# A planned kernel for attention and two expert stages: other task durations and start rules in the planner, the ranking in four tasks, early transposes in other PSUM banks

## The chip, the cores and the metric

The kernel runs on one core of a Trainium2 chip. The metric is the device time of one execution in microseconds (us); lower is better. The kernel before takes 797.78 us (median of 3 runs, 797.66 to 799.06).

## The reference

Three stages follow each other, all in float32. `q`, `k`, `v` have 4 batches, 8 heads, 576 positions and 64 numbers for each head; there are 2304 tokens of 512 numbers.

```python
scores = q @ k.T / sqrt(64) - 2.0**-(head + 1) * abs(i - j)   # only 0 <= i - j < 128
x = softmax(scores) @ v                    # back to (2304, 512)
h = x @ w_in                               # 512 -> 2048
x = (h - tanh(h)) @ w_out                  # 2048 -> 512
logits = cos(x, expert_emb) / tau          # 8 experts
e = argmax(logits); gate = softmax(logits)[e]
out = gate * (relu(x @ w1[e]) @ w2[e])     # for each token, its own expert; 512 -> 1024 -> 512
```

## The kernel before

**The work.** Tokens are in 18 blocks of 128, and two blocks make one of 9 groups (`g`). Attention of a block is done in four quarters of two heads each (`quarter`). The middle stage runs in 72 steps (`step`): one step is one group with two of the 16 column blocks of `w_in` and the rows of `w_out` that answer to them. The first four steps belong to group 0, the next eight to group 1, then come the other four of group 0, and eight for each later group. When a group is done, `route` finds its experts and scatters its rows into a bucket for each expert in HBM. Then eight experts follow (`moe2`, `expert`), with their own weights. Products are made in two or three parts (a rounded high part and the rest), so each float32 operand is split once: the high part is copied by ScalarE (ACT) or VectorE (DVE), the rest is a subtraction on VectorE or GpSimd (POOL).

**The order.** Nothing runs in the order in which it is written. Every piece of work is a task of `Plan`: the engines that could do it with a duration for each, a due time, the keys that it reads and writes, and a PSUM bank that it takes or frees. `Plan.order` is a list scheduler that runs while the program is built: it keeps a time for each engine, takes again and again the task that can start first (ties go to the earlier due time), and puts it on the engine that is expected to finish first. The tasks, sorted by planned start, are then written out in that order, and each engine works through its own list in order. So a duration in the plan doesn't change an instruction; it changes where in its engine's list the instruction stands. On the chip, semaphores hold each instruction until its operands are there.

**A quarter.** `scores` (PE, into the banks `sc0` and `sc1`, or `acc0` and `acc1` for odd quarters below `NALT`), `soft` (VectorE: bias and row minimum, L498), `exp` (ACT, L512). For the first four blocks (`early`) the probabilities are transposed on PE into the single bank `misc` (`tr_pe`, L533), copied out (`tr_out`, L537) and multiplied with `v` (`pv_f`, L547). For all later blocks they are split into float16 parts (`s_hi`, `s_lo`), transposed by a DMA that SP issues (`tr`, L527: `pt<-ph`), and multiplied on PE (`pv`, L558). `x_out` transposes a finished block on PE into `misc` (L645), and ACT (L652) and VectorE (L653) copy it to `xT`, which the first product of a step (`g1`, L693) reads. The second product is `g2` (L717); it reads `gh` and `gl` (L706, L710).

**The routing.** `route` splits a block into three bfloat16 parts (L791, L796), transposes them by one DMA (`turn`, L800: `x3T<-x`) and multiplies them with the embeddings on PE (`lg3`, L805). `choose` and `settle` rank the experts by their number of tokens with some 20 small VectorE instructions in one task each (`ranking`); SP reads the result for the addresses of the experts' weights.

The planner's model of a transfer that SP issues:

```python
free[e] = st + 0.5                     # SP is free again
pipe = max(pipe, st + 1.1) + eng[e]    # the DMA pipe, with the task's own time
end = pipe + 1.0                       # landed
```

Of the kernel before, what the change touches and what calls it, by code (L numbers as in the profile page):

```python
# [24 lines left out]
NT = B * S  # L25
DM = H * D
FF = 2048
E = 8
# [13 lines left out]
LOENG = {"DVE": 0.69}  # L42
LEAD = 2
WLEAD = 1
# [3 lines left out]
NALT = 8  # L48
ALPHA = 1.0
# [21 lines left out]
class Plan:  # L71
# [4 lines left out]
    LAT = {"PE": 0.3, "SP": 0.0, "SW": 0.0}  # L76
# [4 lines left out]
    def add(self, eng, fn, due, r=(), w=(), take=None, free=None):  # L81
# [16 lines left out]
        self.tasks.append((eng, fn, due, deps, take, free))  # L98

    def order(self, places):  # L100
# [8 lines left out]
        pipe = 0.0  # L109
# [3 lines left out]
        while cand:  # L113
# [8 lines left out]
            for n in cand:  # L122
                eng, fn, due, _, take, _ = T[n]
# [5 lines left out]
                fin = {e: max(free.get(e, 0.0), r0) + c + ALPHA * load.get(e, 0.0) for e, c in eng.items()}  # L129
                e = min(fin, key=fin.get)  # L130
                st = max(free.get(e, 0.0), r0)
# [6 lines left out]
            eng, fn, _, _, take, rel = T[n]  # L138
            if take:
                avail[take].remove(min(avail[take]))  # L140
            if e == "SP":
                free[e] = st + 0.5
                pipe = max(pipe, st + 1.1) + eng[e]
                end = pipe + 1.0
            elif e == "SW":
                free["POOL"] = max(free.get("POOL", 0.0), st) + 1.04
                free[e] = st + eng[e]
                end = st + eng[e] + 2.0
            else:
                end = free[e] = st + eng[e]  # L150
            lat = self.LAT.get(e, 0.15)
# [14 lines left out]
class Builder:  # L166
# [64 lines left out]
    def consts(self, P):  # L231
# [8 lines left out]
        for h in range(H):  # L240
            P.add({"DVE": 0.2} if h < 2 else {"POOL": 0.5}, lambda e, h=h: self.eng(e).tensor_scalar(
# [67 lines left out]
    def weight(self, P, kind, f, due):  # L309
# [35 lines left out]
        P.add({"DVE": 0.47, "ACT": 0.62}, top, due, r=[raw], w=[zk])  # L345
        P.add({"DVE": 0.69}, rest, due, r=[raw, zk, "at"], w=[wf])
        P.add({"ACT": 0.62, "DVE": 0.47}, hi, due, r=[wf, "at"], w=[raw, (key, 0)])
# [6 lines left out]
    def qk_half(self, P, b, hf, due):  # L354
# [27 lines left out]
        sub = {"POOL": 1.23, "DVE": 0.6}  # L382
        if b >= NF - 1:
            k, kh = ("k", b, hf), ("kh", s, hf)
            P.add({"SP": 0.73}, lambda e: load("k"), due - 2, r=["at"], w=[k, "stk"])
            P.add({"ACT": 0.52}, kcopy, due, r=["at", k, "stk"], w=[kh])
            P.add(sub, ksub, due, r=["at", kh, "stk"], w=[("kl", s, hf)])
        if b >= NF:
            q, qn = ("q", b, hf), ("q", n)
            P.add({"SP": 0.73}, lambda e: load("q"), due - 2, r=["at"], w=[q, "stq"])  # L390
            P.add({"ACT": 0.52}, qcopy, due, r=["at", q, "stq"], w=[qn])
            P.add(sub, qsub, due, r=["at", qn, "stq"], w=[("ql", n)])
# [28 lines left out]
    def v_half(self, P, b, hf, due):  # L421
# [5 lines left out]
        def load(e):  # L427
# [4 lines left out]
        sub = {"DVE": 0.34, "POOL": 0.69}  # L432
        P.add({"SP": 0.36}, load, due - 2, r=["at"], w=[("vst", n)])
        P.add({"ACT": 0.31}, lambda e: nc.scalar.copy(out=v[0], in_=st["v"]), due, r=["at", ("vst", n)],
              w=[("vt", s, hf, 0)])
        P.add(sub, lambda e: self.eng(e).tensor_tensor(out=st["v"], in0=st["v"], in1=v[0], op=ALU.subtract), due,
              r=["at", ("vt", s, hf, 0)], w=[("vst", n)])
# [1063 lines left out]
```

## Time and profile before

| what | value |
|---|---|
| time, median of 3 runs | 797.78 us |
| the profiled execution | 795.44 us, of which 793.8 us are its span from the first to the last instruction |
| PE (TensorE) busy in the span | 762.9 us, 96% |
| VectorE, ScalarE, GpSimd busy | 569.4, 419.8, 239.1 us |
| granted clock of TensorE, mean of the span | 0.994 of 2.4 GHz |

All times below are from the start of that span. "Busy" is the time in which an engine has an instruction in work. PE's instructions overlap, so a short hole between two of them can disappear in its busy time; weight loads (PEld) are listed apart. A wait is idle time of an engine just before an instruction, put down to what released it.

### The profile page before, as it was taken

How to read it: one execution, taken by the hardware profiler on the slowest of the kernel's cores; microseconds unless marked ns; L12 is line 12 of the kernel's file. 1: busy time of each engine (PE TensorE's matmuls, PEld its weight loads, DVE VectorE, ACT ScalarE, POOL GpSimd, SP SyncE). 2: the span in 40 equal slices, each digit the busy share in tenths (PEclk: the TensorE clock that was granted, in tenths of full speed). 3: DMA queues.
4: the chain of work that ended last, by engine and by line, in shares of the span. 5: the costliest groups of instructions: out<-in, count | busy, mean ns of one | idle time of the engine just before them, and what ended most of it. 6: DMA issues, size and time to landing. Idle time of an engine off the chain costs nothing.

```text
span 793.8 us, 15243 instructions
## 1 busy us (share of the span) xinstructions
PE 762.9 (96%) x5237; PEld 678.1 (85%) x5237; DVE 569.4 (72%) x1538; ACT 419.8 (53%) x953; POOL 239.1 (30%) x256
## 2 busy tenths in 40 slices
PE   6899999999999999999999999999999999999994
PEld 4789899897988989889989888889779989899993
DVE  5989889977796786887887875875466665666320
ACT  5887875564554544555555633564255545545220
POOL 3231238554353343344424321331200210210210
PEclk9999999999999999999999999999999999999998
DMA  8984278764363363364364433572367656665000
GB/s 308 415 349 123 81 205 239 149 146 96 98 143 86 67 147 87 74 146 101 84 124 108 87 61 92 148 239 81 105 231 232 217 178 203 201 199 175 30 29 30
DMA packets 127416, 117.34 MB, mean 148 GB/s; under 512 B 87885, under 2 KB 91981, under 8 KB 127200
## 3 DMA queue, kind: packets, MB, share of 16 engines
q1 hardware_dynamic: 124304, 106.81, 48.9%
q0 software_dynamic: 3024, 9.46, 3.2%
q8 instruction: 43, 0.70, 0.4%
q14 instruction: 45, 0.37, 0.2%
HBM read 85.81 MB, written 16.56 MB: 129 GB/s over the span
## 4 chain that ended last, share of the span: by engine, by line
PE 61%; DMA 13%; DVE 11%; issue 9%; ACT 2%; POOL 1%; SPq 1%; POOLq 0%; DVEq 0%; ACTq 0%
PE h L693 18%; PE acc L717 16%; PE he L1092 9%; PE y L1127 7%; DMA out<-yo,ix 4%; PE o L558 3%; PE y L1123 2%; DMA rawo<-in_w_out 2%; PE sc L476 2%; DMA x3T<-x 2%; DVE gl L710 2%; DMA est<-in_w 2%; DMA pt<-ph 1%; DMA stk<-in_k 1%; DVE sc L498 1%
## 5 line engine op out<-in xcount | busy, mean ns | idle before, releaser
L693 PE MATMUL h<-xT,wi 128*128 128x256 f32 x1728 | 226.3, 285 | 0.0
L693 PEld LDWEIGHTS h<-xT,wi 128*128 128x128 f32 x1728 | 217.6, 192 | 5.4 <-issue 1.0
L717 PE MATMUL acc<-wo,gh 128*128 128x512 f32 x576 | 184.6, 402 | 0.5 <-DVE x2row L757 0.5
L717 PE MATMUL acc<-wo,gl 128*128 128x512 f32 x288 | 113.1, 393 | 0.0
L717 PEld LDWEIGHTS acc<-wo,gh 128*128 128x128 f32 x576 | 99.0, 189 | 15.0 <-DVE x2row L757 0.7
L698 ACT ACTIVATE t<-h 128x512 f32<-128x512 f32 x72 | 43.0, 598 | 93.4 <-PE h L693 85.5
L1127 PE MATMUL y<-eo,ge 128*128 128x512 f32 x336 | 88.8, 399 | 0.3 <-ACT ge L1108 0.3
L512 ACT ACTIVATE p<-sc,mx 128x256 f32<-128x256 f32 (+1 forms) x128 | 59.3, 464 | 43.1 <-DVE mx L498 37.7
L1152 POOL DMA_INDIRECT out<-yo,ix x23 | 23.5, 1020 | 189.9 <-ACT yo L1148 40.2
L710 DVE TENSOR_TENSOR gl<-t,gh 128x512 fp32r<-128x512 f32 x72 | 67.5, 937 | 5.7 <-ACT gh L706 4.8
L1127 PEld LDWEIGHTS y<-eo,ge 128*128 128x128 f32 x336 | 59.5, 188 | 10.6 <-ACT ge L1108 0.6
L498 DVE CUSTOM_DVE_ANT_0 sc<-sc,bias 128x256 f32<-128x256 f32 (+1 forms) x136 | 49.5, 373 | 23.7 <-PE sc L476 20.0
L1025 DVE TENSOR_TENSOR eo<-est,eo 128x512 fp32r<-128x512 f32 x61 | 44.6, 736 | 29.5 <-ACT eo L1021 27.9
L717 PEld LDWEIGHTS acc<-wo,gl 128*128 128x128 f32 x288 | 54.1, 188 | 12.7 <-DVE gl L710 0.7
L1021 ACT CAST eo<-est 128x512 fp32r<-128x512 f32 x64 | 39.5, 620 | 36.9 <-PE y L1123 18.4
L701 DVE TENSOR_TENSOR t<-h,t 128x512 f32<-128x512 f32 x72 | 49.4, 687 | 13.3 <-ACT t L698 13.2
L1114 DVE SCALAR_TENSOR_TENSOR ge<-he,ge 128x256 fp32r<-128x256 f32 x104 | 28.7, 316 | 40.8 <-ACT ge L1108 39.8
L1092 PEld LDWEIGHTS he<-xA,ei 128*128 128x128 f32 x384 | 54.2, 188 | 2.5
L1092 PE MATMUL he<-xA,ei 128*128 128x288 f32 (+2 forms) x384 | 56.1, 295 | 0.0
L1108 ACT ACTIVATE ge<-he 128x288 fp32r<-128x288 f32 (+2 forms) x56 | 23.1, 414 | 61.5 <-PE he L1092 55.9
L522 POOL TENSOR_TENSOR ph<-p,ph 128x512 f16<-128x512 f32 (+1 forms) x33 | 38.3, 1160 | 56.9 <-ACT ph L517 41.6
L1092 PEld LDWEIGHTS he<-xT,ei 128*128 128x128 f32 x384 | 53.4, 189 | 2.1
(208 smaller groups left out, 1325.9 us busy)
## 6 DMA issues: line engine op xcount, KB each, us to landing
est<-in_w SPq DMA_DIRECT2D x128, 256.0 KB
rawi<-in_w_in SPq DMA_DIRECT2D x16, 511.8 KB
rawo<-in_w_out SPq DMA_DIRECT2D x16, 511.8 KB
stk<-in_k SPq DMA_DIRECT2D x30, 256.0 KB
stq<-in_q SPq DMA_DIRECT2D x28, 256.0 KB
bucket<-in_c_pad SPq DMA_DIRECT2D x8, 771.0 KB
xe<-bucket SPq DMA_DIRECT2D x17, 257.0 KB
vst<-in_v SPq DMA_DIRECT2D x30, 128.0 KB
```

What stands on the lines that cost most here:

```text
L498: nc.vector.tensor_tensor_reduce(out=x, in0=x, in1=self.bias[:, h, c0:c1], scale=-0.125, scalar=mx[:, 1:2] if m else 3.0e38, op0=ALU.add, ...
L512: nc.scalar.activation(out=v["p32"][:, jj * W:(jj + 1) * W], in_=x, func=AF.Exp, scale=-1.0, bias=v["mx"][jj][:, 0:1], accum_out=self.sums ...
L522: self.eng(e).tensor_tensor(out=ph[:, 2 * W:4 * W], in0=v["p32"][:, 0:2 * W], in1=ph[:, 0:2 * W], op=ALU.subtract)
L693: nc.tensor.matmul(h3(v["h"], f2), lhsT=w[:, a, k, :], rhs=xT[c][:, :, k, :], start=(k == 0 and n == 0), stop=(k == KD - 1 and n == 2))
L698: nc.scalar.activation(out=v["t"], in_=v["h"].rearrange("p a b -> p (a b)"), func=AF.Tanh)
L701: nc.vector.tensor_tensor(out=v["t"], in0=v["h"].rearrange("p a b -> p (a b)"), in1=v["t"], op=ALU.subtract)
L710: self.eng(e).tensor_tensor(out=v["gl"], in0=v["t"], in1=v["gh"].bitcast(F32), op=ALU.subtract)
L717: nc.tensor.matmul(self.acc[g, t], lhsT=v[a][:, c0:c0 + 128], rhs=self.w["o", fs[f2]][:, c, :], start=(first and f2 == 0 and n == 0), stop ...
L1021: nc.scalar.copy(out=t[:, 0, :], in_=v["x"])
L1025: self.eng(eng).tensor_tensor(out=t[:, 1, :], in0=v["x"], in1=t[:, 0, :].bitcast(F32), op=ALU.subtract)
L1092: nc.tensor.matmul(h[:, 0:N], lhsT=w[:, a, c0:c0 + 128], rhs=xT()[b][:, k, 0:N], start=(k == 0 and n == 0), stop=(k == KD - 1 and n == 2))
L1127: nc.tensor.matmul(y[t], lhsT=gt(f, a)[:, (t - ts[0]) * 128:(t - ts[0] + 1) * 128], rhs=self.w["o", f0 + f][:, b, :], start=(f == 0 and n ...
```

## The change

It edits the planner and the tasks' declarations. The arithmetic and the number of instructions stay as they are.

- Nearly all task durations get other values, most of them larger: a step's `g1` 1.285 to 1.425, its `g2` 0.643 to 0.69, `tanh` 0.48 to 0.63, the subtractions 0.60 to 0.72, the weight casts on ACT 0.62 to 0.81, `pv` 0.53 to 0.56.
- Tasks get a `late` value. The two kinds of DMA transposes (`tr` and `turn`) have `late=2.5`: what they produce is planned as ready 2.5 later, and SP is planned as taken for 1.25. For other transfers SP is planned as free after 0.4 in place of 0.5.
- Tasks get a `port` flag. While the last planned GpSimd task runs, a flagged task isn't planned to start on VectorE. Flagged are the weights' `top`, `rest` and `hi`, the subtractions of `qk_half` and `v_half`, `recip`, a step's `lo` (`gl`), and in `route` the scaling and the casts.
- The latency between tasks is 0.05 in place of 0.15, and 0.2 in place of 0.3 behind PE.
- Odd quarters below 8 transpose into the bank `h1`, and `x_out` of blocks 0 and 1 into `h0`; these banks are used by `g1` from the first steps on.
- `choose` and `settle` are cut into several tasks with their own due times: the keys, `ranks`, `order`, `places`, and what follows. The instructions are the same.

```diff
-LOENG = {"DVE": 0.69}
+LOENG = {"DVE": 0.72}
+LATE = 2.5
+NOWN = 8
+NXO = 2
-    LAT = {"PE": 0.3, "SP": 0.0, "SW": 0.0}
+    LAT = {"PE": 0.2, "SP": 0.0, "SW": 0.0}
...
+                at = {e: max(free.get(e, 0.0), r0) for e in eng}
+                if port and "DVE" in at and pool[0] <= at["DVE"] < pool[1]:
+                    at["DVE"] = pool[1]
+                fin = {e: at[e] + c + ALPHA * load.get(e, 0.0) for e, c in eng.items()}
...
-                free[e] = st + 0.5
-                pipe = max(pipe, st + 1.1) + eng[e]
-                end = pipe + 1.0
+                free[e] = st + (1.25 if late else 0.4)
+                pipe = max(pipe, st + 1.0) + eng[e]
+                end = pipe + 0.9
...
-            lat = self.LAT.get(e, 0.15)
+                if e == "POOL":
+                    pool = (st, end)
+            lat = self.LAT.get(e, 0.05) + late
...
-            v["tp"] = self.misc()
+            v["tp"] = self.misc(f"h{own}" if own is not None else "misc")
...
-        P.add({"SP": 0.5 if one else 0.9}, tr, due, r=["at", ("ph", a % 2), ("ph", a % 2, 1)], w=[("pt", a % 2)])
+        P.add({"SP": 0.7 if one else 1.2}, tr, due, late=LATE, r=["at", ("ph", a % 2), ("ph", a % 2, 1)], w=[("pt", a % 2)])
...
+        own = 0 if b < NXO else None
+        hb = [("h", own)] if own is not None else []
...
-            v["ps"] = self.misc()
+            v["ps"] = self.misc(f"h{own}" if hb else "misc")
...
-            P.add({"PE": 1.285}, lambda e, f2=f2: g1(f2), due, ...
+            P.add({"PE": 1.425}, lambda e, f2=f2: g1(f2), due, ...
-        P.add({"DVE": 0.6}, lo, due - 20, r=["t", gh], w=[gl])
+        P.add({"DVE": 0.72}, lo, due - 20, r=["t", gh], w=[gl], port=True)
...
-            P.add({"SP": 1.35}, lambda e, t=t: turn(t), due, r=[("x3", n) for n in range(3)], w=["x3T", ("wz", 1)])
+            P.add({"SP": 1.55}, lambda e, t=t: turn(t), due, late=LATE, r=[("x3", n) for n in range(3)], w=["x3T", ("wz", 1)])
...
-        P.add({"DVE": 2.4}, pick, due, r=["cps", "con", "small"], w=["big", "first", ("ids", 0)], free="misc")
+        P.add({"DVE": 0.4}, start, due, r=["cps", "con", "small"], w=["first", "rank"], free="misc")
+        self.ranking(P, due, 0)
+        P.add({"DVE": 0.8}, pick, due, r=["rank"], w=["big", "first"])
...
+        P.add({"DVE": 1.0}, ranks, due, r=["con"], w=["rank"])
+        P.add({"DVE": 0.7}, order, due, r=["con"], w=["rank"])
+        P.add({"DVE": 0.5}, places, due, r=["rank"], w=[("ids", n)])
...
-        P.add({"DVE": 2.6}, fix, due, r=["cps", "con", "small"], w=["first", "cap", ("ids", 1)], free="misc")
+        P.add({"DVE": 0.4}, start, due, r=["cps", "con", "small"], w=["first", "rank"], free="misc")
+        self.ranking(P, due, 1)
+        P.add({"DVE": 1.3}, fix, due + 1, r=["rank"], w=["cap", "key2"])
+        P.add({"DVE": 0.2}, least, due + 1, w=["cap"])
```

## Rows read from the trace of the kernel before

**Rows 1.** Windows: span in us, then busy us (instructions) of each engine, PEclk, DMA share, GB/s.

```profile
0.00:60.00 60.00, 49.77 (x336) 40.39 (x337) 47.54 (x146) 44.44 (x119) 20.78 (x48) 1.00 0.94 357
60.00:540.00 480.00, 471.81 (x3470) 422.24 (x3469) 390.83 (x1054) 269.63 (x629) 183.79 (x177) 1.00 0.51 123
540.00:783.00 243.00, 241.00 (x1436) 215.53 (x1434) 131.01 (x340) 105.09 (x206) 33.52 (x31) 1.00 0.47 150
...
20.00:40.00 20.00, 16.13 (x132) 14.28 (x132) 17.98 (x52) 17.96 (x45) 5.39 (x6) 1.00 1.03 415
```

**Rows 2.** Waits of PE from 60 to 545 us: total us, times, longest us.

```profile
PE o L558 <- DMA pt<-ph: 2.7, 3, 1.7
PE misc L805 <- DMA x3T<-x: 2.3, 4, 0.9
PE o L558 <- DVE gl L710: 1.1, 1, 1.1
PE misc L1365 <- DVE cum L873: 0.7, 1, 0.7
PE acc L717 <- DVE x2row L757: 0.5, 1, 0.5
PE misc L805 <- DVE xT L653: 0.5, 1, 0.5
PE misc L846 <- DVE oh L836: 0.3, 1, 0.3
```

**Rows 3.** Waits of PE in the first 60 us.

```profile
PE sc L470 <- DMA kf<-in_k: 4.3, 1, 4.3
PE sc L470 <- ACT p L512: 3.1, 3, 1.7
...
PE misc L645 <- ACT ptf L537: 0.6, 1, 0.6
PE misc L533 <- DVE xT L653: 0.4, 1, 0.4
```

**Rows 4.** Windows of 2 us from 294 to 300 us; PEclk is third from the end.

```profile
294.00:296.00 2.00, 1.67 (x26) 1.67 (x27) 0.94 (x6) 0.00 (x0) 1.08 (x1) 0.95 0.96 307
296.00:298.00 2.00, 2.00 (x11) 2.00 (x11) 1.58 (x13) 0.22 (x1) 0.00 (x0) 0.50 0.73 142
298.00:300.00 2.00, 2.00 (x17) 1.96 (x16) 0.00 (x0) 0.15 (x1) 0.00 (x0) 0.70 0.00 0
```

**Rows 5.** The chain that ended last, in order of time: start us, us, what.

```profile
151.68 4.92 DMA pt<-ph
...
183.31 4.76 DMA x3T<-x
...
223.86 2.83 DMA stq<-in_q
...
453.63 3.08 DMA pt<-ph
...
510.10 1.78 DVE x L796
```

**Rows 6.** Instructions on the tile pt, their ns (least/median/most), and who waited for it.

```profile
L527 SPq DMA_TRANSPOSE pt<-ph x56: 1189/1232/2398, 81.9 to 483.1; - x56
...
  PEld L558: 7.4, 10
```

**Rows 7.** Instructions on the tile gl: VectorE's subtraction of a step, ns least/median/most.

```profile
L710 DVE TENSOR_TENSOR gl<-t,gh x72: 661/692/1811, 41.8 to 539.2; 128x512 fp32r<-128x512 f32 x72
```

**Rows 8.** Timeline of VectorE at two borders between groups: start us, us.

```profile
151.15 0.68 DVE L653 TENSOR_TENSOR xT<-misc,xT 128x512 fp32r<-128x512 f32 x1
206.65 0.68 DVE L653 TENSOR_TENSOR xT<-misc,xT 128x512 fp32r<-128x512 f32 x1
```

**Rows 9.** Timeline of PE at the same two borders: the next group's first product.

```profile
152.28 1.92 PE L693 MATMUL h<-xT,wi 128*128 128x256 f32 x14
...
208.81 1.59 PE L693 MATMUL h<-xT,wi 128*128 128x256 f32 x12
```

## The prediction before the change was built

> **What bounds the kernel now.** I read the windows first, by stage. Between 60 and 540 us PE is busy for 471.8 of 480 us, from 540 to 783 us for 241.0 of 243 us; in the first 60 us it is idle for 10.2 us, and after 783 us the span has 10.8 us in which the last rows leave the chip [rows 1]. So TensorE is the bound, and a new order of the same instructions can win only PE's holes: 8.2 us in the middle, 2.0 us in the experts, and some of the 10.2 us ahead. Nothing in the change touches the last 10.8 us.
>
> Next come PE's own waits, which say whose the holes are. In the middle seven kinds make 8.1 of the 8.2 us [rows 2]. Three waits for the transposes of the probabilities (2.7 us, the longest 1.7) and four for those of the routing (2.3 us) are 5.0 us. VectorE's `gl` makes 1.1 us, its `cum` 0.7, `x2row` 0.5, `xT` 0.5 and `oh` 0.3. At the start, 4.3 us wait for the first load and 3.1 us for the first exponentials; only 0.6 + 0.4 = 1.0 us are waits of a transpose for the shared bank `misc` [rows 3].
>
> Then the granted clock, which busy time doesn't show. It is 0.95, 0.50 and 0.70 in three windows of 2 us from 294 us on, and 1.00 in all the stages around [rows 4, 1]. A level of 0.50 is 1.2 in place of 2.4 GHz. PE had just stood still for its longest wait in the middle, the 1.7 us for `pt` [rows 2]. The price is 2 x (0.05 + 0.50 + 0.30) = 1.7 us, on top of the hole.
>
> **The change, part by part.** No instruction is added or removed, so each part is worth what the new order does to these holes.
>
> *Later transposes.* The old plan lets `pt` land 1.1 + 0.9 + 1.0 = 3.0 us after SP starts; the new one says 1.0 + 1.2 + 0.9 + 2.5 = 5.6 us. The chain shows 4.92 and 3.08 us for `pt`, and 4.76 us for `x3T` [rows 5]. So 3.0 was too little by up to 1.9 us, and 5.6 is above all of them. SP is held for 1.19 to 2.40 us by one transpose [rows 6], where the old plan said 0.5 and the new one says 1.25. The plan will put at least one more product ahead of `pv` and `lg3`. The margin of 2.5 us is above the longest of these waits, 1.7 and 0.9 us [rows 2], so all seven could close. I take 4.0 of the 5.0 us, because the operands of a transpose can be late too. Bounds: nothing, if the holes only move; and 7.4 us, the idle time of the weight loads that wait for `pt` alone [rows 6], if PE's busy time hides part of the loss.
>
> A rule of the Trainium skill speaks against this part. The Trainium skill, Advanced Engine Details and Errata, section X-Bar Transpose (TRN2), says that such transposes are as fast as ordinary transfers. A plain load took 2.83 us in the same chain, against 3.08 and 4.92 [rows 5]: one of the two transposes agrees, the other doesn't. By the rule the old 3.0 was right, the added 2.5 corrects nothing, and this term would be 0.
>
> *The clock.* With the wait of 1.7 us gone there is nothing here that slows the clock: 1.7 us. Bounds 0 and 1.7.
>
> *True durations and the port rule.* VectorE's subtraction for `gl` takes 692 ns at the median and up to 1811 [rows 7], where the old plan has 0.6. The new plan has 0.72 and doesn't start it beside GpSimd. That bears on the `gl` wait (1.1 us) and, by better times in general, on the other 2.0 us of [rows 2]. I take 1.0 of the 3.1 us, between 0 and 3.1: the flag is on only some of VectorE's work. The routing's own subtraction, which has no flag, took 1.78 us at 510 us [rows 5].
>
> The Trainium skill, SBUF — State Buffer, section Who interferes with whom, says that a VectorE instruction with two SBUF inputs and a GpSimd instruction that reads SBUF block each other for a whole instruction. The 1811 ns agree in kind [rows 7]. By that rule the unflagged subtractions go on colliding, as with my 1.0; a plan that flagged them all could aim at 3.1.
>
> *Banks.* The odd early quarters and the first two `x_out` no longer queue for `misc`: 1.0 us [rows 3]. From 20 to 40 us VectorE is busy for 17.98 and ACT for 17.96 of 20 us [rows 1], so the two copy engines, not the banks, limit the start. Bounds 0 and 5.9 us, which is the idle 10.2 us without the first load's 4.3. The new readers of `h0` and `h1` stand ahead of `g1`, which needs their results anyway; no wait is added that isn't there by the data.
>
> *Ranking in tasks.* The VectorE work is the same; other subtractions may slip in between. It lies where PE's whole idle time is the 0.7 us behind `cum` [rows 2] and the 2.0 us of the experts [rows 1]. I take 0; the bounds are a loss and a gain of 2.0 us. SP's reading of the ranks waits for the same instructions as before. If the cover goes, the experts' loads behind that reading are late next.
>
> *What goes the other way.* The old plan has little room at the borders between groups. At two of them `xT` is done at 151.83 and 207.33 us, and the next group's `g1` starts at 152.28 and 208.81 [rows 8, 9]: 0.45 and 1.48 us. Five of the eight borders are of this kind, with room of 0 to 1.5 us. A `pv` that is planned later makes `x_out` later. Late next are `xT`, then `g1` of a whole group, and behind it in PE's list all that follows. Five borders that are each short of 2.5 us, with about 0.75 us of room on average, are 5 x 1.75 = 8.75 us; nothing is the lower bound, since products of the old group can fill. I take 2.0 us, because an order by true durations shifts `pv` by about one product, not by the whole 2.5.
>
> Sum: -4.0 - 1.7 - 1.0 - 1.0 + 0 + 2.0 = -5.7 us. The profiled execution was 795.44 us, its span 793.8 and 1.6 around it; it would be 789.7. The median of the runs stands 2.3 us higher, at 797.78, and gives **792.1 us**, 0.7% less.
>
> **The rivals.** A change of 0.2%, 1.6 us, is about what a measurement of this kernel can tell from none.
>
> *The borders pay it all back (slower).* The planned lateness of 2.5 us reaches `xT` in full. Then the transposes and the clock still give 5.7 us and nothing else does, and the borders cost 8.75: 797.8 - 5.7 + 8.75 = 800.8 us. For it: the 0.45 us at 151.83 [rows 8, 9]. Against it: the PE products of the old group that can go ahead of `g1`, and that a quarter's delay doesn't add up over the quarters. It decides when the borders lose more than 5.7 + 1.6 = 7.3 us, an average of 1.5 us at each of five.
>
> *The transposes were not late; the holes move (no change).* The landing of 3.08 us beside the planned 3.0 speaks for it, that of 4.92 us against it [rows 5]. The rule of the Trainium skill above speaks for it too. PE then waits elsewhere for the same late `ph` or `x`. The clock may still be saved: 797.8 - 1.7 + about 1 for other holes = 797.1 us.
>
> *The start gains as well (much faster).* PE's 5.9 us ahead close for a good part because attention has more banks in flight, and the middle loses all 8.2 us with the clock's 1.7: 797.8 - 8.2 - 1.7 - 4 = 783.9 us. Against it stand the 90% of both copy engines from 20 to 40 us [rows 1].
>
> **How the numbers follow.** The forecast, 789 to 796 us, has 0.55; much faster 0.16; no change 0.12; slower 0.17. So faster by over 0.2%: 0.55 + 0.16 = 0.71; the same 0.12; slower 0.17. The range reaches into both outer cases, from 784.5 us, near the third rival, to 799.5 us, which takes in no change and half of the border's case; about 0.18 is left out. The likeliest case's own range is 789 to 796 us.
>
> **What would show it.** Right: the waits of PE for `pt` and `x3T` fall from 5.0 us to about 1; the clock stays at 1.00 around the routing; PE's idle time from 60 to 540 us falls from 8.2 to about 4 to 5 us; `gl` stays nearer to 0.69 us. The banks: the two waits of a transpose at the start are gone, and the first `g1` is not later. Wrong: waits of `g1` (L693) for `xT` of over a microsecond at the borders, or a new wait of over 1.5 us in the middle, which brings the clock down again. If the first products of the steps start some microseconds later than before while VectorE is full, the new durations have moved work to the wrong engine, and the forecast fails at the start.

## The result and the profile after

The changed kernel takes 808.09 us (median of 4 runs, 807.45 to 811.74); the kernel before took 798.42 us beside it. The ratio is 1.011 (95% interval 1.0075 to 1.0147): slower, where 0.7% faster was forecast. The profiled execution took 808.58 us, with a span of 806.9 (before 795.44 and 793.8). Line numbers are about 10 to 40 higher now: `g1` is L707, `gl` L724, `pv` L568, `lg3` L819, `oh` L850, the subtraction of the experts' weights L1065.

The windows of the changed kernel, first by stage as in [rows 1], then two short stretches:

```profile
0.00:60.00 60.00, 53.40 (x322) 41.99 (x323) 42.44 (x134) 40.76 (x113) 19.15 (x47) 0.97 0.92 352
60.00:540.00 480.00, 469.12 (x3421) 422.10 (x3420) 371.20 (x1008) 269.22 (x626) 229.81 (x218) 0.99 0.50 119
540.00:796.00 256.00, 251.10 (x1496) 223.66 (x1496) 132.30 (x342) 111.41 (x215) 52.73 (x45) 1.00 0.47 151
20.00:40.00 20.00, 19.83 (x150) 16.82 (x148) 15.30 (x51) 15.61 (x44) 4.26 (x5) 1.00 1.03 416
...
296.00:298.00 2.00, 2.00 (x19) 2.00 (x18) 1.17 (x4) 1.27 (x3) 1.62 (x3) 1.00 1.32 73
...
524.00:526.00 2.00, 0.00 (x0) 0.00 (x0) 1.90 (x6) 1.75 (x4) 1.12 (x1) 1.00 0.47 162
526.00:528.00 2.00, 0.53 (x6) 0.53 (x7) 1.93 (x5) 0.02 (x1) 1.38 (x2) 0.71 0.68 229
528.00:530.00 2.00, 2.00 (x6) 1.52 (x6) 1.85 (x7) 1.74 (x3) 1.28 (x1) 0.50 0.48 158
```

Three things are to be seen. GpSimd (the last busy column) went from 183.79 to 229.81 us between 60 and 540 us [rows 1], while VectorE fell from 390.83 to 371.20. PE's idle time in that stage grew from 8.2 to 10.9 us. And the clock, which is 1.00 where it had been 0.50 [rows 4], is 0.50 at three other places now, one of them just behind a stretch in which PE did nothing.

PE's waits from 60 to 545 us (as [rows 2]), and those of the experts' start:

```profile
PE misc L860 <- DVE oh L850: 4.0, 2, 3.8
PE sc L486 <- ACT p L522: 3.0, 4, 1.1
PE misc L290 <- DVE ec L285: 1.5, 1, 1.5
PE acc L731 <- DVE gl L724: 0.7, 2, 0.5
PE o L568 <- DMA pt<-ph: 0.5, 1, 0.5
...
PE h L707 <- DVE xT L667: 0.4, 2, 0.2
...
PE y L1163 <- DVE yo L1179: 1.1, 1, 1.1
PE y L1167 <- DVE yo L1186: 0.9, 1, 0.9
```

The waits for transposes, 5.0 us before, are 0.5 us. In their place stand a wait of 3.8 us for the one-hot of the routing (`oh`, which marks each token's expert), 3.0 us of waits for the exponentials, 1.5 us for the embeddings (`ec`), and behind 600 us two for the experts' outputs.

Where the time goes is seen best from the start of the first product (`g1`) of a step, cut into four lengths (us, from the profiled execution of each kernel). Steps count from 0; "to 24" is the time at which step 24 starts. All kernels of this study stand in the table; each ratio is to executions of the kernel before that ran beside it.

| kernel | ratio to before (95%) | to 24 | 24 to 64 | 64 to 71 | 71 to end |
|---|---|---|---|---|---|
| before | 1 | 208.8 | 284.3 | 41.0 | 259.7 |
| changed | 1.0111 (1.0075 to 1.0147) | 218.3 | 279.6 | 46.0 | 263.0 |
| changed, old durations | 1.0055 (1.0024 to 1.0085) | 215.4 | 279.5 | 40.6 | 261.7 |
| changed, no lateness | 1.0146 (1.0102 to 1.0189) | 219.0 | 284.6 | 42.6 | 260.2 |
| changed, no port rule | 1.0174 (1.0154 to 1.0195) | 222.9 | 279.8 | 44.9 | 262.8 |
| changed, shared bank | 1.0023 (1.0000 to 1.0045) | 212.1 | 277.8 | 46.2 | 264.4 |
| changed, old latencies | 1.0026 (1.0004 to 1.0047) | 218.2 | 275.8 | 42.8 | 261.5 |
| changed, one latency back | 1.0072 (1.0043 to 1.0100) | 220.0 | 280.2 | 38.0 | 268.5 |
| changed, one duration by 0.01 | 1.0083 (1.0056 to 1.0110) | 218.9 | 277.8 | 43.5 | 263.1 |
| changed, weights not on GpSimd | 0.9969 (0.9949 to 0.9990) | 220.8 | 280.1 | 38.1 | 259.4 |
| changed, weights with port flag | 1.0172 (1.0108 to 1.0236) | 217.4 | 280.4 | 45.9 | 265.0 |
| old latencies + weights not on GpSimd | 0.9983 (0.9961 to 1.0004) | 219.8 | 276.2 | 38.4 | 262.5 |
| shared bank + weights not on GpSimd | 0.9937 (0.9915 to 0.9959) | 218.0 | 277.7 | 38.2 | 261.4 |
| before + ranking | 1.0008 (0.9983 to 1.0033) | 213.0 | 281.9 | 44.4 | 259.3 |
| before + durations | 0.9993 (0.9968 to 1.0017) | 213.0 | 280.3 | 43.5 | 262.4 |
| before + lateness | 1.0084 (1.0058 to 1.0110) | 221.6 | 280.2 | 38.8 | 261.8 |
| before + port rule | 0.9935 (0.9903 to 0.9967) | 213.6 | 275.8 | 42.2 | 260.2 |
| before + banks | 1.0007 (0.9990 to 1.0023) | 212.5 | 279.8 | 44.7 | 260.0 |
| before + latencies | 1.0136 (1.0094 to 1.0179) | 216.5 | 287.3 | 42.7 | 259.9 |
| before + port rule + weights not on GpSimd | 0.9929 (0.9901 to 0.9957) | 215.0 | 276.2 | 40.5 | 260.3 |

Against before the changed kernel is 9.5 us behind at step 24, wins 4.7 us from 24 to 64, and loses 5.0 and 3.3 us after that: 13.1 us in the spans. One profile is not exact: where two or three kernels have the same planned order up to some place (changed, weights not on GpSimd, weights with port flag; before and before + ranking; and each kernel beside its own version without the weights on GpSimd), step 24 differs by up to 5.9 us between them, but the length from 24 to 64 by 0.8 at most (2.4 for before, whose clock slowed down there). More than half of that arises ahead of the first `g1`, which starts at 32.1 to 34.8 us in one order (changed), at 35.0 and 37.5 us in another (before), at 33.1 and 36.9 us in a third (shared bank). From the first `g1` to step 24 profiles of one order agree within 2.1 us: 185.4 to 186.0 us (changed), 173.8 and 175.5 us (before), 179.0 and 181.1 us (shared bank).

### The profile page after: what moved, and what is told of

The parts are those of the page before. It is cut to its first block, busy times and chain, and to the rows that moved or that the text cites. A ratio compares the mean times of both kernels' runs of the same rounds, so it can differ in the third digit from the quotient of the medians.

```text
span 806.9 us, 15291 instructions
## 1 busy us (share of the span) xinstructions
PE 774.4 (96%) x5237; PEld 688.0 (85%) x5237; DVE 545.9 (68%) x1484; ACT 422.1 (52%) x953; POOL 302.7 (38%) x310
## 5 line engine op out<-in xcount | busy, mean ns | idle before, releaser
L707 PE MATMUL h<-xT,wi 128*128 128x256 f32 x1728 | 228.7, 286 | 1.6 <-DVE wi L346 0.8
L707 PEld LDWEIGHTS h<-xT,wi 128*128 128x128 f32 x1728 | 219.0, 192 | 8.0 <-DVE wi L346 1.2
L731 PEld LDWEIGHTS acc<-wo,gh 128*128 128x128 f32 x576 | 102.2, 192 | 16.1 <-issue 0.7
L731 PE MATMUL acc<-wo,gl 128*128 128x512 f32 x288 | 114.8, 399 | 0.7 <-DVE gl L724 0.7
L522 ACT ACTIVATE p<-sc,mx 128x256 f32<-128x256 f32 (+1 forms) x128 | 59.1, 463 | 42.2 <-DVE mx L508 25.1
L724 DVE TENSOR_TENSOR gl<-t,gh 128x512 fp32r<-128x512 f32 x72 | 64.4, 895 | 13.2 <-ACT gh L720 12.7
L1167 PEld LDWEIGHTS y<-eo,ge 128*128 128x128 f32 x336 | 59.5, 188 | 10.7 <-issue 1.1
L532 POOL TENSOR_TENSOR ph<-p,ph 128x512 f16<-128x512 f32 (+1 forms) x37 | 43.6, 1178 | 62.0 <-ACT ph L527 45.5
L1065 POOL TENSOR_TENSOR ei<-est,ei 128x512 fp32r<-128x512 f32 x16 | 20.6, 1289 | 111.1 <-ACT ei L1061 106.6
L380 POOL TENSOR_TENSOR khl<-stk,khl 64x512 fp32r<-64x512 f32 x28 | 37.5, 1338 | 59.8 <-ACT khl L376 50.9
L1132 PE MATMUL he<-xT,ei 128*128 128x288 f32 (+2 forms) x384 | 54.9, 295 | 0.0
L1192 POOL DMA_INDIRECT out<-yo,ix x23 | 24.7, 1074 | 80.2 <-ACT yo L1188 38.8
```

Source lines behind the costliest of these rows:

```text
L380: self.eng(e).tensor_tensor(out=k, in0=r4("k")[64:128], in1=k.bitcast(F32), op=ALU.subtract)
L522: nc.scalar.activation(out=v["p32"][:, jj * W:(jj + 1) * W], in_=x, func=AF.Exp, scale=-1.0, bias=v["mx"][jj][:, 0:1], accum_out=self.sums ...
L532: self.eng(e).tensor_tensor(out=ph[:, 2 * W:4 * W], in0=v["p32"][:, 0:2 * W], in1=ph[:, 0:2 * W], op=ALU.subtract)
L707: nc.tensor.matmul(h3(v["h"], f2), lhsT=w[:, a, k, :], rhs=xT[c][:, :, k, :], start=(k == 0 and n == 0), stop=(k == KD - 1 and n == 2))
L724: self.eng(e).tensor_tensor(out=v["gl"], in0=v["t"], in1=v["gh"].bitcast(F32), op=ALU.subtract)
L731: nc.tensor.matmul(self.acc[g, t], lhsT=v[a][:, c0:c0 + 128], rhs=self.w["o", fs[f2]][:, c, :], start=(first and f2 == 0 and n == 0), stop ...
```

## The experiments

All kernels named "before +" have the ranking in tasks. The texts speak of these theories: A, the new durations harm; B, the port rule harms, because it moves subtractions to GpSimd; C, the lateness is paid at the borders between groups; D, any other plan scatters the time by some us; E, the banks delay the first steps; F (later), the smaller latencies harm.

**The changed kernel with one part undone.** Old durations (all task durations go back, of which two are shown; the new tasks of the ranking keep theirs):

```diff
-LOENG = {"DVE": 0.72}
+LOENG = {"DVE": 0.69}
...
-            P.add({"PE": 1.425}, lambda e, f2=f2: g1(f2), due, ...
+            P.add({"PE": 1.285}, lambda e, f2=f2: g1(f2), due, ...
```

> The changed kernel with the task durations of before; late, port, banks, latencies and the ranking in tasks stay. Theory A (the new durations hold the copies and transposes of the start back, and make GpSimd look cheap): the loss is gone, 790 to 798 us, and the first 100 us win back about 7 us. Theory B (the port rule moves subtractions to GpSimd, where they block VectorE): 804 to 808 us. Theory C (the lateness of 2.5 eats the borders): 804 to 808 us. Theory D (any change of the plan scatters the time by some us): anything from 793 to 808 us, with the holes in new places.

Measured: 801.45 us, ratio 1.0055. Half of the loss comes back, and step 64 to 71 takes 40.6 us, as in the kernel before (41.0).

No lateness:

```diff
-LATE = 2.5
+LATE = 0.0
```

> The changed kernel with late=0 for the DMA transposes. Theory C: the time falls to about 798 us or below. Theories A and B: the middle loses its gain of about 5 us again (waits for pt and x3T return to 3 to 5 us), 810 to 813 us. Theory D: anything from 800 to 813 us.

Measured: 809.94 us, 1.0146. The time is 1.9 us longer, less than the 2.6 us that a change without meaning moves (below), so it doesn't show that the lateness helps in this set. PE's waits do change. Those for transposes, from 60 to 545 us in this kernel:

```profile
PE o L568 <- DMA pt<-ph: 6.6, 8, 2.1
PE misc L819 <- DMA x3T<-x: 2.5, 2, 1.8
```

9.1 us of waits for transposes against 0.5 in the changed kernel, and 5.0 us more from step 24 to 64.

No port rule:

```diff
-        self.tasks.append((eng, fn, due, deps, take, free, late, port))
+        self.tasks.append((eng, fn, due, deps, take, free, late, False))
```

> The changed kernel without the port rule. Theory B: the hole of 3.8 us behind oh and the holes behind yo are gone, 800 to 803 us. Theory A: the start stays as slow, 806 to 810 us. Theory D: anything from 800 to 812 us.

Measured: 813.15 us, 1.0174: 5.1 us worse still, so the rule helps and B falls.

Early transposes in the shared bank again:

```diff
-NOWN = 8
-NXO = 2
+NOWN = 0
+NXO = 0
```

> The changed kernel with all early transposes in misc again. Theory A, B, C: the first product starts 2 to 3 us later and the time is 808 to 811 us. A theory E, that the banks themselves delay the first steps because g1 waits for h0 and h1: the start is faster by 3 us or more, 802 to 805 us.

Measured: 802.34 us, 1.0023. The banks cost 0.9% in this set; step 24 starts 6.2 us earlier in this profile. From 64 to 71 nothing comes back (46.2 us), and PE waits 4.4 us for `oh` there.

**The kernel before with one part alone.** The new durations (all of them again; one is shown):

```diff
-LOENG = {"DVE": 0.69}
+LOENG = {"DVE": 0.72}
```

> The kernel before with the ranking in tasks and the new durations alone. Theory A (the durations do the harm): 803 to 810 us with a slow start and holes behind VectorE. Theories B and C: 792 to 799 us. Theory D: anything from 793 to 808 us.

Measured: 798.76 us, 0.9993: nothing. The lateness:

```diff
+LATE = 2.5
...
-                free[e] = st + 0.5
+                free[e] = st + (1.25 if late else 0.5)
...
-            lat = self.LAT.get(e, 0.15)
+            lat = self.LAT.get(e, 0.15) + late
```

> The kernel before with the ranking in tasks and late=2.5 (with SP held for 1.25) alone. The prediction's own step: waits of PE for pt and x3T fall from 5.0 us to about 1, 792 to 795 us. Theory C: the borders lose more than that, 799 to 803 us.

Measured: 805.52 us, 1.0084, although PE's waits for `pt` from 60 to 545 us are 0.2 us in all and those for `x3T` are gone. Where it loses, by windows (columns as in [rows 1]), and PE's waits from 160 to 200 us:

```profile
170.00:180.00 10.00, 6.70 (x51) 5.54 (x49) 5.78 (x25) 4.61 (x13) 6.96 (x7) 1.00 0.56 132
180.00:190.00 10.00, 8.00 (x26) 6.46 (x27) 4.32 (x11) 3.20 (x9) 2.33 (x3) 0.51 0.63 170
```

```profile
PE misc L659 <- DVE xr L601: 2.4, 1, 2.4
...
PE acc L731 <- DVE x2row L771: 1.3, 1, 1.3
...
```

In this profile the loss sits in one tangle of 20 us, in which PE is idle for 5.3 us, and in the half clock behind it. No `g1` waits for `xT` there, as C would have it; the longest wait is that of `x_out` for `xr`, one link ahead of `xT`.

The port rule:

```diff
+                if port and "DVE" in at and pool[0] <= at["DVE"] < pool[1]:
+                    at["DVE"] = pool[1]
```

> The kernel before with the ranking in tasks and the port rule alone. Theory B: GpSimd takes some 20 more tasks, unflagged VectorE work collides with them, 800 to 805 us. Otherwise: VectorE's gl is steadier, 795 to 798 us.

Measured: 793.49 us, 0.9935, the best of the single parts. From 200 to 500 us this is all that is left of PE's waits; it keeps the old transposes and has no half clock before the end:

```profile
PE o L568 <- DMA pt<-ph: 0.7, 1, 0.7
PE misc L860 <- DVE oh L850: 0.2, 1, 0.2
```

The banks:

```diff
+NOWN = 8
+NXO = 2
```

> The kernel before with the ranking in tasks and the banks alone. The prediction's own step: 796 to 798 us, with the first product some us earlier. Theory E (g1 waits for h0 and h1): 800 us or more.

Measured: 799.35 us, 1.0007. The first `g1` starts at 29.8 us, in place of 35.0 (37.5 in the second profile of that order), but step 24 at 212.5: an earlier start isn't kept.

So far the parts didn't add up. The latencies, which the prediction had not weighed, came next, with a probe for D and one for the hole at 523 us. In the first of these kernels `late` is 0 for all tasks.

```diff
-    LAT = {"PE": 0.3, "SP": 0.0, "SW": 0.0}
+    LAT = {"PE": 0.2, "SP": 0.0, "SW": 0.0}
...
-                free[e] = st + 0.5
-                pipe = max(pipe, st + 1.1) + eng[e]
-                end = pipe + 1.0
+                free[e] = st + (1.25 if late else 0.4)
+                pipe = max(pipe, st + 1.0) + eng[e]
+                end = pipe + 0.9
...
-            lat = self.LAT.get(e, 0.15)
+            lat = self.LAT.get(e, 0.05) + late
```

> The kernel before with the ranking in tasks and only the planner's latencies and transfer constants of the change (0.05 in place of 0.15 between engines, 0.2 in place of 0.3 behind TensorE, and the three numbers of the transfer model); its plan gives a step's first product up to 5 us earlier than the plan of the kernel before. Theory F (the smaller latencies let the plan put a reader straight behind its producer, so that real waits stand ahead of ready work): slower than before, ratio 1.004 to 1.010, with more waits of TensorE and of ScalarE and VectorE for each other. Theory D (every change of the plan scatters the time by some us, whatever it is): a ratio anywhere in 0.993 to 1.008, with waits at the known places (137 to 145, 173 to 190, 517 to 537 us). If the latencies do nothing: 0.998 to 1.002.

Measured: 809.87 us, 1.0136: alone, this part costs as much as the whole change. PE's waits from 60 to 545 us:

```profile
PE o L568 <- DMA pt<-ph: 8.0, 7, 2.3
PE misc L819 <- DMA x3T<-x: 2.7, 4, 1.1
PE sc L486 <- ACT p L522: 2.7, 3, 1.3
PE misc L659 <- DVE xr L598: 1.7, 1, 1.7
```

The waits for transposes are 10.7 us, twice those of before [rows 2]. So about half of what the lateness removes in the changed set (from 9.1 to 0.5 us) is there because of the rest of the set: before has 5.0 us.

The changed kernel with the old latencies (the same lines, from + to -; transposes still hold SP for 1.25):

> The changed kernel with the old latencies and the old transfer constants (transposes still hold the sync engine for 1.25). Theory F: half of the loss or more comes back, ratio to before 1.000 to 1.006. Theory D: any ratio in 0.998 to 1.015, not tied to the latencies. If the latencies do nothing in this set: 1.009 to 1.013, as the changed kernel.

Measured: 801.58 us, 1.0026. Most of the loss comes back; PE still waits 2.8 us for `oh` behind 500 us.

One planned duration by 0.01:

```diff
-LOENG = {"DVE": 0.72}
+LOENG = {"DVE": 0.73}
```

> The changed kernel with one planned duration 0.72 written as 0.73 (the last subtraction of the weights, which VectorE alone does); nothing about the hardware is truer or falser by it, yet 1249 of the 3363 places in the planned order differ and 69 tasks change their engine. Theory D: the time moves by more than 2 us either way from the changed kernel's 808, the holes appear at other places or with other lengths. Theories A, C, E, F (each part of the change has a cost of its own): the time stays at 807 to 810 us, ratio to before 1.009 to 1.013, with the same holes.

Measured: 805.52 us, 1.0083. D holds to its size: 2.6 us for a change without meaning. It is no excuse for the 10 us, and the hole behind `oh` is there as well (2.8 us at 525 us).

The experts' weights on VectorE alone:

```diff
-        P.add({"DVE": 0.72, "POOL": 1.32}, lo, due, r=[st, (key, 0)], w=[(key, 1)])
+        P.add({"DVE": 0.72}, lo, due, r=[st, (key, 0)], w=[(key, 1)])
```

> The changed kernel with the experts' weight subtractions on VectorE alone in place of VectorE or GpSimd; the planned order is the same up to 482 us, so only the stretch behind it can differ. If the wait of 3.8 us at 523 us (a product that waits for the routing's one-hot, behind VectorE's slow subtractions beside GpSimd) and the half clock after it come from that collision: both vanish and the time is 803 to 805 us, ratio 1.004 to 1.008. If VectorE's 24 us of added subtractions cost more than the collision: the wait stays or moves later, with waits for the expert weights behind 540 us, and the time is 808 to 812 us.

Measured: 797.44 us, 0.9969. This one edit turns the change from 1.1% slower to 0.3% faster, more than twice what was expected of it. The windows from 500 to 545 us of the kernel before, the changed one and this one:

```profile
500.00:545.00 45.00, 43.39 (x297) 38.51 (x296) 36.17 (x74) 26.85 (x49) 13.51 (x11) 1.00 0.66 198
```

```profile
500.00:545.00 45.00, 40.60 (x268) 35.81 (x267) 32.19 (x55) 23.81 (x43) 23.05 (x18) 0.92 0.59 175
```

```profile
500.00:545.00 45.00, 44.35 (x312) 39.80 (x311) 35.43 (x78) 26.16 (x47) 7.51 (x6) 1.00 0.67 207
```

GpSimd's busy time is 13.51, 23.05 and 7.51 us; PE's goes the other way: 43.39, 40.60 and 44.35. That isn't a rule for every order: with the old durations it is 13.98 and 41.27 us, without the lateness 19.58 and 43.25. But the four kernels without these weights on GpSimd have PE at 43.9 to 44.6 us, and of the sixteen others one (the lateness alone, 44.51) has over 43.4.

How it happens in the changed kernel is seen in its timeline (start, length), of VectorE with the instruction ahead of the routing's chain, of GpSimd, of ScalarE, and of PE's products of the logits (`lg3`):

```profile
521.26 1.36 DVE L724 TENSOR_TENSOR gl<-t,gh 128x512 fp32r<-128x512 f32 x1 [1.58 <-ACT gh L720]
522.55 0.17 DVE L824 TENSOR_REDUCE lg<-misc 128x8 f32<-128x24 f32 x1
523.04 1.29 DVE L1065 TENSOR_TENSOR ei<-est,ei 128x512 fp32r<-128x512 f32 x1 [0.32 <-ACT ei L1061]
...
524.95 1.24 DVE L848 TENSOR_TENSOR eq<-eq,con 128x16 f32<-128x16 f32 x1
526.23 0.17 DVE L849 TENSOR_REDUCE rs<-eq 128x2 f32<-128x16 f32 x1
526.43 0.98 DVE L850 TENSOR_TENSOR oh<-con,rs 128x16 bf16<-128x16 f32 x1
...
524.88 1.28 POOL L1065 TENSOR_TENSOR eo<-est,eo 128x512 fp32r<-128x512 f32 x1 [1.11 <-ACT eo L1061]
526.13 1.25 POOL L1065 TENSOR_TENSOR ei<-est,ei 128x512 fp32r<-128x512 f32 x1
...
520.09 0.62 ACT L1061 CAST ei<-est 128x512 fp32r<-128x512 f32 x1 [2.61 <-DMA est<-in_w]
...
519.51 0.46 PE L819 MATMUL misc<-en,x3T 128*128 128x24 bf16 x12
```

and the same work with the weights on VectorE alone:

```profile
524.12 0.17 DVE L824 TENSOR_REDUCE lg<-misc 128x8 f32<-128x24 f32 x1
524.22 0.68 DVE L1065 TENSOR_TENSOR ei<-est,ei 128x512 fp32r<-128x512 f32 x1
...
525.52 0.17 DVE L848 TENSOR_TENSOR eq<-eq,con 128x16 f32<-128x16 f32 x1
...
525.93 0.18 DVE L850 TENSOR_TENSOR oh<-con,rs 128x16 bf16<-128x16 f32 x1
...
522.87 0.46 PE L819 MATMUL misc<-en,x3T 128*128 128x24 bf16 x12
```

An instruction on 16 columns takes 1.24 us and one 0.98 us, where they take 0.17 and 0.18 alone: each ends 0.03 us behind a GpSimd instruction (524.88 + 1.28 = 526.16 against 526.19; 527.38 against 527.41). From the first of these rows to the end of `oh` it is 4.86 us against 1.99 (525.93 + 0.18 - 524.12), with one weight subtraction in between in both. These 2.9 us are three quarters of PE's wait of 3.8 us for `oh`. Behind it the clock is at 0.50 for 6.8 us.

The stretched instructions aren't all of it. In the kernel before, `oh` was stretched as well, beside a GpSimd subtraction, and PE didn't wait for it there, since 3.1 us of `g1` stood ahead of its reader:

```profile
517.52 1.00 DVE L836 TENSOR_TENSOR oh<-con,rs 128x16 bf16<-128x16 f32 x1
...
517.19 1.30 POOL L1025 TENSOR_TENSOR eo<-est,eo 128x512 fp32r<-128x512 f32 x1 [5.86 <-ACT eo L1021]
```

In the changed kernel the chain also begins late: `lg3` is done at 519.97 us, but VectorE's L824 starts at 522.55. Ahead of it in VectorE's list stands `gl`, which waited 1.58 us for ScalarE's `gh`; and ScalarE had first waited 2.61 us for a load of weights. With the weights on VectorE alone the chain begins 0.8 us behind `lg3` (523.33 to 524.12). The one edit removes both, and no run tells them apart.

The Trainium skill, SBUF — State Buffer, section Who interferes with whom, says that a VectorE instruction with two SBUF inputs contends with a GpSimd instruction that reads SBUF, and that a reduction never does. This agrees: the two-input L848 and L850 are stretched, the reduction L849 runs beside GpSimd's instruction of 526.13 in 0.17 us.

**The same edit in other orders, and the last part alone.** With the old latencies:

> The changed kernel with the old latencies and transfer constants, and with the experts' weight subtractions on VectorE alone; both edits won singly (ratio 1.0026 and 0.9969, from 1.0111). If they act in different stretches (the first 200 us, and 500 to 640 us): both gains stay, 1.0026 less about 0.7% (the hole of 2.8 us for the one-hot at 523 us and the half clock behind it), ratio 0.992 to 0.997, and TensorE loses under 2 us from 500 to 545 us. If the late gain depended on the order of the one plan: the ratio stays at 1.000 to 1.004, with a hole elsewhere behind 500 us.

Measured: 797.52 us, 0.9983. From 64 to 71 it takes 38.4 us, with the hole gone, but the two gains don't add up: 4.1 us in the medians (801.58 to 797.52), where 10.7 us came from the same edit without the old latencies. Both acted on the stretch behind 500 us; the old latencies had brought 3.2 and 1.5 us there, and 3.8 us between steps 24 and 64, of which this kernel's median shows nothing.

With the port rule alone:

> The kernel before with the ranking in tasks, the port rule alone, and the experts' weight subtractions on VectorE alone. The port rule alone gave 0.9935 and shows no hole behind 500 us that is longer than 0.9 us. If GpSimd's share is bad only where it makes such a hole: the same, 0.992 to 0.996. If VectorE is too full without GpSimd: slower, 0.996 to 1.002, with waits for expert weights behind 540 us. If the share is bad in any order: faster, under 0.991.

Measured: 792.75 us, 0.9929, the same as without the edit (793.49). Where GpSimd's share makes no hole, it costs nothing that can be measured.

The changed kernel with only the latency between engines back:

```diff
-            lat = self.LAT.get(e, 0.05) + late
+            lat = self.LAT.get(e, 0.15) + late
```

> The changed kernel with the latency between engines back at 0.15 (behind TensorE it stays 0.2, the transfer constants stay new). If the latency between engines is the harmful number: most of what the undo of all latencies gave comes back, ratio 1.001 to 1.006, and TensorE's loss from 60 to 100 us falls from 3.9 to about 1 us. If it is the transfer constants or the 0.2: the ratio stays at 1.008 to 1.013. The scatter of one small change was 0.3% (one planned duration by 0.01), so a ratio in between decides nothing by itself.

Measured: 804.36 us, 1.0072: in between, 3.7 us from the changed kernel, where a change without meaning moves 2.6 us. Which of the five numbers of this part does the harm stays open.

The kernel before with the ranking in tasks:

> The kernel before with the ranking cut into tasks and nothing else; its planned order is that of the kernel before up to 425 us. If the cut only lets other subtractions slip in between, as the prediction had it: 0.998 to 1.002. If it makes the ranks later, and so the loads of the experts' weights: slower by 2 us or more, 1.002 to 1.005, with waits behind 500 us.

Measured: 800.29 us, 1.0008: nothing.

**Bank and weights undone together:**

> The changed kernel with the early transposes back in the shared bank and the experts' weight subtractions on VectorE alone. Singly these gave 1.0023 and 0.9969, from 1.0111. If the first acts ahead of 200 us and the second behind 500 us (the steps by 24 were 6 us earlier with the shared bank, and TensorE's loss behind 500 us was 9.6 us in that order): both gains stay, ratio 0.986 to 0.993, under the kernel before. If they are two tries at the same loss, as the old latencies turned out to be: 0.995 to 1.001.

Measured: 794.92 us, 0.9937, faster than the kernel before, and just outside the slow end of what was expected if both gains stay (0.986 to 0.993). The weights' edit gives 7.4 us here (802.34 to 794.92), the bank's 2.5 us on top of it (797.44 to 794.92). Step 24 starts at 218.0 us here, and at 212.1 us with the shared bank alone, in the same order up to there. So that profile's 6.2 us were no proof of where the bank acts. From the first `g1` on, both shared-bank kernels are 4 to 7 us shorter up to step 24 than the changed order (179.0 and 181.1 against 185.4 to 186.0), which points to that stretch.

The port flag on the experts' weights:

```diff
-        P.add({"DVE": 0.72, "POOL": 1.32}, lo, due, r=[st, (key, 0)], w=[(key, 1)])
+        P.add({"DVE": 0.72, "POOL": 1.32}, lo, due, r=[st, (key, 0)], w=[(key, 1)], port=True)
```

> The changed kernel with the port flag on the experts' weight subtractions as well; the planned order is the same up to 490 us, and three more of them are planned on GpSimd. If the collisions are the harm: the hole behind the one-hot shrinks, ratio 1.002 to 1.007. If GpSimd's longer instruction and its queue are the harm (its results come late, so the buffers and the next loads are late): the same or slower than the changed kernel, 1.009 to 1.015, with the hole of 3 us or more.

Measured: 811.28 us, 1.0172, above both ranges, with the hole as it was (3.9 us for `oh`). The flag moves more to GpSimd (29.22 us from 500 to 545 us) and doesn't guard the small instructions of the chain, which have no flag. The expectation set the collisions against GpSimd's queue; that the hole stays doesn't decide between them, because the collisions stay too, at other instructions. `oh` takes 0.18 us here, but three ahead of it are stretched:

```profile
523.23 1.04 DVE L828 TENSOR_TENSOR lg<-lg,rs 128x16 f32<-128x16 f32 x1
...
524.51 1.26 DVE L846 TENSOR_TENSOR eq<-lg,rs 128x16 f32<-128x16 f32 x1
525.80 1.19 DVE L847 TENSOR_TENSOR lg<-lg,rs 128x16 f32<-128x16 f32 x1
```

## Why the prediction was wrong

**The later transposes: the waits were right, their worth wasn't settled.** 4.0 of 5.0 us were forecast. The waits fell to 0.5 us, and with the lateness removed the steps 24 to 64 took 5.0 us more. But about half of that only pays for what the rest of the set adds, and alone the lateness closed the same waits and made the kernel 0.8% slower. By the rule of the Trainium skill (Advanced Engine Details and Errata, section X-Bar Transpose (TRN2)) this term would have been 0; the waits went, so the old plan did expect the transposes too early. The rule is on the speed of the transfers, which no run here measures apart from their landing.

**The clock: right at its place, its price not settled.** At 294 to 300 us it is 1.00. It is 0.50 at three new places for 17.1 us in all. By the prediction's way of pricing that is 8.5 us. The runs of the changed kernel don't bear this out: a mean granted clock of 0.985 went with 808.58 and 811.74 us, and 0.993 with 807.45. The 0.008 between them is 6.5 us of an 806.9 us span at full speed; the time moved by 1.1 and 4.3 us. But these are three runs, and two of them differ by 3.2 us at the same clock.

**The step that failed** is the premise under all parts, that each "is worth what the new order does to these holes", and with it the term "True durations and the port rule", 1.0 us with bounds "between 0 and 3.1". It priced the holes that were there and allowed no loss. Undoing each in the set shows that the durations cost 6.6 us there (808.09 to 801.45) and that the port rule gives 5.1 us (808.09 to 813.15).

By stretches, the sum had the start 1.0 us shorter, the middle 4.7 us shorter (-4.0 - 1.7 - 1.0 + 2.0), and nothing behind. The profiles show 9.5 us more up to step 24, 4.7 us less from 24 to 64, and 8.3 us more behind that. That the middle agrees to the tenth is luck: the stretches aren't the same, and against the second profile of before's order (281.9 us) the gain is 2.3 us.

What the premise missed behind step 64 is that a duration decides which engine gets a task, too. GpSimd's instructions went from 256 to 310, its busy time from 239.1 to 302.7 us. Of the 128 subtractions for the experts' weights it did 15 in the kernel before, 33 in the changed one, and 17 in that one with the old durations. From 500 to 545 us, in the changed kernel, 15 weight subtractions were there:

```profile
L1065 POOL TENSOR_TENSOR eo<-est,eo 128x512 fp32r<-128x512 f32 x8 | 12.4, 1560 | 8.7 <-ACT eo L1061 8.7
L1065 POOL TENSOR_TENSOR ei<-est,ei 128x512 fp32r<-128x512 f32 x7 | 9.0, 1288 | 11.1 <-ACT ei L1061 6.6 <-PE acc L731 4.5
...
L724 DVE TENSOR_TENSOR gl<-t,gh 128x512 fp32r<-128x512 f32 x7 | 7.5, 1078 | 6.1 <-ACT gh L720 6.0
```

and in the kernel before 8:

```profile
L1025 POOL TENSOR_TENSOR ei<-est,ei 128x512 fp32r<-128x512 f32 x6 | 8.5, 1427 | 13.2 <-ACT ei L1021 13.2
L1025 POOL TENSOR_TENSOR eo<-est,eo 128x512 fp32r<-128x512 f32 x2 | 2.6, 1294 | 12.1 <-ACT eo L1021 12.1
```

The prediction had the collision in its rows (`gl` up to 1811 ns, [rows 7]) and said that unflagged subtractions go on colliding; it missed that more of them would, in the stretch where the routing's chain of small VectorE instructions feeds PE. Keeping them off GpSimd is worth 10.7 us in the medians (808.09 to 797.44), all of it behind step 64 in the profiles (309.0 to 297.5 us); the start stays as late as it was (220.8 us at step 24). The durations are the part that sends them there: with the old ones step 64 to 71 is 5.4 us shorter (46.0 to 40.6).

That isn't enough by itself. The durations alone put 30 of the 128 on GpSimd, 11 of them in that stretch, and the time didn't change (798.76 us). What the weights' edit is worth depends on the order: 10.7 us in the changed kernel, 7.4 with the shared bank, 4.1 with the old latencies, 0.7 with the port rule alone.

The port rule itself was under-priced: alone it gives 5.4 us (793.49 against 798.85 for the kernel before beside it), and the steps 24 to 64 take 275.8 us in place of 281.9 or 284.3. In the full set it is worth about as much, 5.1 us, but not in that stretch (279.6 us with it, 279.8 without); there step 24 starts at 218.3 us with it and 222.9 without.

**The latencies were not weighed at all.** The change lists them, and the sum has no term for them. Undone, they give 6.5 us back (808.09 to 801.58); alone they are 1.4% slower. That smaller values let the plan put a reader too close behind its producer fits the doubled waits above, but is argued, not shown.

**The banks** were forecast at 1.0 us of gain, with no loss possible. Undone in the set they give 5.8 us back (808.09 to 802.34); alone they change nothing. The two waits of a transpose at the start are gone, and the first `g1` came at 32.3 in place of 35.0 us. But profiles of one order differ there by as much, and the kernel with the shared bank has 33.1. Alone, the banks bring it to 29.8 us, and nothing of that is left by step 24. So the third rival's early start came only there, and was lost again.

**The ranking** alone cost nothing, as forecast.

**The borders** fell as a mechanism, both as the term of 2.0 us and as the slower rival: `g1` waits for `xT` for 0.4 us in all. What the lateness alone loses sits in one tangle at 170 to 190 us. The slower rival's 800.8 us was nearer to the result than the forecast, for a reason that it didn't give.

**What stays open** is the start, where the largest part of the loss lies in the profiles (9.5 us): the kernels with the changed set are at 215 to 223 us at step 24 (one profile: 212), those with one part at 212 to 222, before at 209 and 213. The prediction named late first products as a sign that the new durations had moved work to the wrong engine while VectorE is full. The sign came, but not its reason: with the old durations step 24 is still at 215.4 us, and VectorE was less busy than before (15.30 of 20 us from 20 to 40 us, where it had 17.98). From the first `g1` to step 24 the changed order takes 10 to 12 us more than the order of before (185.4 to 186.0 against 173.8 and 175.5), so this is no scatter. The banks, the latencies and the lateness each move it, and the runs don't say by which instructions.

## What to carry to other kernels

In a planned kernel a duration is also a choice of engine: before pricing such an edit, count the instructions that each engine gets and look at what else runs on the engine's shared port at the points where a chain of short instructions feeds the engine that bounds the kernel. Undo each part of a bundle as well as doing it alone: here the durations and the banks cost nothing alone, and yet undoing the durations, the banks or the latencies in the set gives back 6.6, 5.8 or 6.5 us, together twice the loss of 9.7, so the parts can't be added. The best version was the smallest: the port rule alone (with the ranking in tasks), 0.65% faster than before.

## What the hardware showed that was not expected

VectorE instructions of 0.17 us on 128 x 16 elements took 0.98 and 1.24 us beside a GpSimd subtraction, ending 0.03 us behind it. VectorE's subtraction `gl` has the median of before (693 ns, 692 in [rows 7]), but its longest took 3070 ns in place of 1811, although the plan now has the port flag on it:

```profile
L724 DVE TENSOR_TENSOR gl<-t,gh x72: 679/693/3070, 40.9 to 550.3; 128x512 fp32r<-128x512 f32 x72
```

TensorE's clock fell to 0.50 behind a hole of 3.8 us, at 144.6 us behind holes of 1.5 and 0.6 us, and at 55.8 us, where the last hole before it was 0.55 us long.
